# Linear attention and an ELU feed-forward layer on one core: flat attend visits, dummy matmuls in the first batch, and a new order of the work

## The chip, the core and the metric

The kernel runs on one core of a Trainium2 chip. The metric is the device time of one execution in microseconds (us). A core has five engines that run side by side, each with its own queue worked off in order: TensorE (PE, matrix products into the eight PSUM banks), VectorE (DVE), ScalarE (ACT), GpSimd (POOL), and SyncE (SP), which here only starts transfers. POOL and ACT start transfers too; POOL starts those of the weights.

## What is computed

```python
def _attn_ref(q, k, v):                      # each 8 batches x 8 heads x 576 x 64, f32
    q_s = np.exp(q - np.max(q, axis=-1, keepdims=True))
    q_s = q_s / (np.sum(q_s, axis=-1, keepdims=True) + 1e-09)
    k_s = np.exp(k - np.max(k, axis=2, keepdims=True))
    k_s = k_s / (np.sum(k_s, axis=2, keepdims=True) + 1e-09)
    kv = np.einsum('bhsd,bhse->bhde', k_s, v)
    return np.einsum('bhsd,bhde->bhse', q_s, kv)

def _moe_ref(x, w_in, w_out):                # x: 4608 x 512, w_in: 512 x 2048, w_out: 2048 x 512
    h = x @ w_in
    g = np.where(h > 0.0, h, np.exp(np.minimum(h, 0.0)) - 1.0)
    return g @ w_out
```

x is the attention's output with the heads side by side: 8 batches of 576 rows, 512 columns.

## The kernel before

**Blocks.** The 4608 rows of x are worked off in nine blocks j. Blocks 0 to 7 are the first 512 rows (`SM`) of each batch; the remaining 64 rows (`SR`, "the rest") of all eight batches are collected in `XTR` and make block 8. Each block has 16 steps s, one for each 128 hidden columns. A step is: `hidden` (L708, four matmuls L728 of 512 columns into one of three PSUM banks, then the exponential on ACT, L716, and a -1 on POOL, L717, both in the buffer ES), the projection of three steps before (`project`, L749, four matmuls into the banks 3 to 6, `LAG` = 3), and `elu` (L739, DVE: max and min of the bank and ES into GT). A hidden matmul needs the bank that the elu of three steps before has read; a projection needs GT of its step and its piece of W2. After the 16th projection of a block the four banks are evicted (L757 ACT, L759 DVE) and stored.

**Attention.** Beside the steps of block j stands the attention of batch n = j + 1, cut into words that are written by hand into tables: `FIRST` (L42, beside block 0), `SECOND` (L60, block 1), `LATER` (L78, blocks 2 to 6, with `CHANGED` for block 2). A table has three texts for a step: the words behind `hidden`, behind `project` and behind `elu`. `do` (L803) issues them in that order. A word appends its instructions to the queues of their engines, so the order of the words is the order in every queue. `START` (L33) is the list for batch 0, before the steps begin.

The words that matter here (a third field names the engine where it can be chosen; without it qsub, ksub and qmul are POOL's, vconv and the exponentials ACT's):

- `load:X:i:part` starts a transfer of Q, K or V of batch j + i in SP's queue; part A and B are halves, M both, R the rest. `w1:a:b` and `w2:a:b` start transfers of weight columns (or rows) a to b in POOL's queue. `hold` makes SP wait for the last hidden matmul issued, `await:sp:KEY` for the last writer of a tile.
- Q: `qmax` (DVE), `qsub`, `qexp`, `qsum` (DVE, L588 and L590), `qmul` (L602, into QS as f16; `qmulr` for the rest, POOL), then `turn` (a transposing transfer in SP's queue, L618 and L622) and `wide` (ACT, into QT; the rest into QTR). In the first batches `pturn` and `pwide` do this on PE and ACT instead.
- K: in batches 0 to 2 the maximum over rows goes through `kmax`, `kturn`, `kacross`, `diag`, `kspread`, `copy`; later through `peak`, `join`, `kout`, `kin` (a small transfer to memory and back). Then `ksub` and `kexp`. Batch 0 has it as matmuls into PSUM (`kraw` copies K into a bank, `kmin` subtracts the maximum, the exponential reads the bank).
- `vconv` casts V to bf16 (VB), `kv` (L519, 40 matmuls) makes the product, `kfac` (L540, DVE) scales it into the four tiles MB.
- `att:f` (L668) multiplies MB[f] with the 512 columns of QT[f] into bank 7, and `xc:f` copies it to `XT` (L681 ACT, or DVE). `rest0` (L683) does it for the 64 rest columns of all four f in the next block, and `rcopy0` copies those to `XTR`. Suffix 0 in a word means batch j, 2 means batch j + 2.

**Dummy matmuls.** `warm:times:bank` (L862) multiplies a tile of ones into a bank that nobody reads. `START` has one, `warm:4:6`, ahead of all else on PE.

**Waits.** `op` (L141) makes an instruction wait for the last writers of what it reads and for the last writers and readers of what it writes, tile by tile.

## Time and profile before

| what | value |
|---|---|
| median of 3 runs (lowest, highest) | 316.19 us (315.69, 319.87) |
| the profiled execution | 315.58 us |
| its span, first to last instruction | 313.8 us |
| PE busy | 301.7 us, 96% of the span |
| first projection (L749) starts at | 27.81 us |
| a block in the steady part (175.69 to 207.27) | 31.58 us |
| the last projections end, and the last stores | near 310.6 us, 313.8 us |

In the profile, "L728" is line 728 of the kernel above. PEld is TensorE's weight load, which runs beside its matmuls. A timeline row gives start, duration, engine, line, operation, output and input, shape, the number of instructions merged, and in brackets how long the engine sat idle ahead of it and what released it. Durations of neighbouring rows overlap a little, so costs in a row of instructions are taken from start to start.

### The profile page before, as it was taken

How to read it: one execution, taken by the hardware profiler on the slowest of the kernel's cores; microseconds unless marked ns; L12 is line 12 of the kernel's file. 1: busy time of each engine (PE TensorE's matmuls, PEld its weight loads, DVE VectorE, ACT ScalarE, POOL GpSimd, SP SyncE). 2: the span in 40 equal slices, each digit the busy share in tenths (PEclk: the TensorE clock that was granted, in tenths of full speed). 3: DMA queues.
4: the chain of work that ended last, by engine and by line, in shares of the span. 5: the costliest groups of instructions: out<-in, count | busy, mean ns of one | idle time of the engine just before them, and what ended most of it. 6: DMA issues, size and time to landing. Idle time of an engine off the chain costs nothing.

```text
span 313.8 us, 4535 instructions
## 1 busy us (share of the span) xinstructions
PE 301.7 (96%) x1606; PEld 239.1 (76%) x1606; DVE 230.5 (73%) x383; ACT 192.7 (61%) x319; POOL 190.1 (61%) x237
## 2 busy tenths in 40 slices
PE   6778998999999999999999999999999999999995
PEld 3355776688877878887888788888888888888884
DVE  5797996796888979798979897989796353435541
ACT  1675676587856965696569666966696643334432
POOL 1897697468438953995399529952995233333330
PEclk9989999999999999999999999999999999999999
DMA  7999999763796789617951695160512030003003
GB/s 235 327 293 351 382 338 335 178 187 99 193 317 193 178 206 251 207 33 181 304 178 37 186 304 170 36 175 20 167 37 42 0 137 0 0 2 134 0 0 134
DMA packets 65414, 51.35 MB, mean 164 GB/s; under 512 B 29296, under 2 KB 57712, under 8 KB 65392
## 3 DMA queue, kind: packets, MB, share of 16 engines
q1 hardware_dynamic: 57984, 41.23, 47.3%
q0 software_dynamic: 6384, 8.39, 10.9%
q10 hardware_dynamic: 1024, 1.45, 1.6%
q8 instruction: 12, 0.20, 0.3%
q14 instruction: 10, 0.08, 0.1%
HBM read 38.01 MB, written 9.45 MB: 151 GB/s over the span
## 4 chain that ended last, share of the span: by engine, by line
PE 86%; DMA 8%; POOL 3%; DVE 1%; ACT 1%; issue 0%
PE bank L749 40%; PE bank L728 40%; DMA W2S<-in_moe_w_out_dram 6%; PE bank L672 2%; DMA KR<-in_k_dram 1%; PE bank L465 1%; PE bank L529 1%; PE bank L688 1%; POOL QR L578 1%; POOL W1S L247 1%; POOL VB L509 1%; POOL KR L408 1%; PE bank L322 1%; POOL ES L717 0%; PE bank L456 0%; PE bank L533 0%
## 5 line engine op out<-in xcount | busy, mean ns | idle before, releaser
L717 POOL TENSOR_SCALAR ES<-ES 128x512 f32<-128x512 f32 x144 | 100.9, 703 | 105.7 <-ACT ES L716 105.4
L749 PE MATMUL bank<-W2S,GT 128*128 128x512 f32 x576 | 154.6, 392 | 1.6 <-DMA W2S<-in_moe_w_out_dram 1.6
L739 DVE SCALAR_TENSOR_TENSOR GT<-bank,ES 128x512 fp32r<-128x512 f32 x144 | 97.2, 680 | 61.8 <-PE bank L728 44.8
L728 PE MATMUL bank<-XT,W1S 128*128 128x512 f32 x512 | 140.5, 396 | 0.2 <-ACT XT L681 0.2
L716 ACT ACTIVATE ES<-bank 128x512 f32<-128x512 f32 x144 | 85.6, 597 | 77.9 <-PE bank L728 73.9
L749 PEld LDWEIGHTS bank<-W2S,GT 128*128 128x128 f32 x576 | 107.2, 188 | 25.4 <-DVE GT L739 1.6
L728 PEld LDWEIGHTS bank<-XT,W1S 128*128 128x128 f32 x512 | 95.7, 190 | 20.8 <-ACT XT L681 1.1
L578 POOL TENSOR_TENSOR QR<-QR,QM 128x512 f32<-128x512 f32 (+3 forms) x29 | 33.5, 1158 | 7.5 <-DVE QM L570 7.5
L408 POOL TENSOR_TENSOR KR<-KR,NB 128x512 f32<-128x512 f32 x23 | 31.1, 1352 | 0.0
L681 ACT ACTIVATE XT<-bank 128x512 fp32r<-128x512 f32 x31 | 18.4, 598 | 14.8 <-PE bank L672 14.2
L570 DVE TENSOR_REDUCE QM<-QR 128x16 f32<-128x1024 f32 (+3 forms) x18 | 21.7, 1207 | 1.1 <-DMA QR<-in_q_dram 1.0
L588 DVE TENSOR_REDUCE QZ<-QR 128x16 f32<-128x1024 f32 (+3 forms) x18 | 21.7, 1204 | 0.1
L584 ACT ACTIVATE QR<-QR 128x1024 f32<-128x1024 f32 (+3 forms) x18 | 19.1, 1060 | 3.2 <-POOL QR L578 1.7
L602 DVE TENSOR_TENSOR QS<-QR,QI 128x1024 f16<-128x1024 f32 (+1 forms) x15 | 19.8, 1327 | 0.0
L728 PE MATMUL bank<-XTR,W1S 128*128 128x512 f32 x64 | 16.6, 389 | 0.0
L446 ACT ACTIVATE EK<-KR 128x1024 bf16<-128x1024 f32 x14 | 14.7, 1050 | 0.0
L672 PE MATMUL bank<-QT,MB 128*128 128x512 f32 x32 | 13.5, 432 | 0.6 <-DVE MB L550 0.6
L728 PEld LDWEIGHTS bank<-XTR,W1S 128*128 128x128 f32 x64 | 12.0, 188 | 2.5
L511 ACT ACTIVATE VB<-VR 128x1024 bf16<-128x1024 f32 x12 | 12.6, 1049 | 0.0
L662 ACT ACTIVATE QT<-QW 128x1024 fp32r<-128x1024 f16 x12 | 12.5, 1050 | 0.0
L361 DVE TRANSPOSE_TENSOR_REDUCE KM<-KR 128x32 f32<-128x1024 f32 x10 | 12.3, 1234 | 0.0
L515 ACT ACTIVATE VBR<-VR 64x256 bf16<-64x256 f32 x16 | 6.6, 411 | 7.4 <-DMA VR<-in_v_dram 7.2
(85 smaller groups left out, 197.0 us busy)
## 6 DMA issues: line engine op xcount, KB each, us to landing
out_dram<-OSB SPq DMA_DIRECT2D x35, 256.0 KB, 2.9
KR<-in_k_dram SPq DMA_DIRECT2D x7, 1024.0 KB, 8.1
VR<-in_v_dram SPq DMA_DIRECT2D x6, 1024.0 KB, 7.2
QR<-in_q_dram SPq DMA_DIRECT2D x5, 1024.0 KB, 7.1
QR<-in_q_dram SPq DMA_DIRECT2D x6, 512.0 KB, 9.3
VR<-in_v_dram SPq DMA_DIRECT2D x4, 512.0 KB, 6.9
W1S<-in_moe_w_in_dram POOLq DMA_DIRECT2D x1, 1280.0 KB, 12.1
W2S<-in_moe_w_out_dram POOLq DMA_DIRECT2D x1, 1280.0 KB, 10.6
```

The source lines that it names most:

```text
L408: self.op(en, lambda: e.tensor_tensor(kv, kv, m, ALU.subtract), keys + ["NB"], keys)
L570: self.op("dve", lambda: v.tensor_reduce(self.QM[:, g], QR[:, g, :], AX.X, ALU.max), self.qkeys(b, part), self.qstat("QM", part))
L578: self.op(en, lambda: e.tensor_tensor(QR[:, g, :], QR[:, g, :], m, ALU.subtract), keys + self.qstat("QM", part), keys)
L584: self.op("act", lambda: a.activation(QR[:, g, :], QR[:, g, :], AF.Exp), keys, keys)
L588: self.op("dve", lambda: v.tensor_reduce(self.QZ[:, g], QR[:, g, :], AX.X, ALU.add), self.qkeys(b, part), self.qstat("QZ", part))
L602: self.op(en, lambda: e.tensor_tensor(out, src, z, ALU.mult), keys + self.qstat("QI", part), [f"QS{x}" for x in cells])
L672: self.op("pe", lambda: pe.matmul(self.bank[bank][:, :], mb, self.QT[:, f, :], start=True, stop=True), [f"MB{f}", f"QT{part}"], [f"bank{ba ...
L716: self.op("act", lambda: a.activation(ES[:, :], ps, AF.Exp), [f"bank{bank}"], [ek])
L717: self.op("gp", lambda: g.tensor_scalar(ES[:, :], ES[:, :], -1.0, 1.0, ALU.add, ALU.mult), [ek], [ek])
L728: return pe.matmul(ps, self.W1S[:, kc, c * 128:(c + 1) * 128], x[:, kc, :], start=(kc == 0), stop=(kc == 3))
L739: self.op("dve", lambda: v.scalar_tensor_tensor(self.GT[n % NG][:, :], ps, 0.0, ES[:, :], ALU.max, ALU.min), [f"bank{bank}", ek], [f"GT{n ...
L749: return pe.matmul(self.bank[OB[t]][:, :], self.GT[n % NG][:, t * 128:(t + 1) * 128], self.W2S[:, c, :], start=(c == 0), stop=(c == NCH - 1))
```

## The change

Three parts. First, from batch 2 on the four `att` words and the rest become five flat visits: the 4 x 576 columns of the attention's output are cut at `CUTS`, and each visit fills one bank with one or two matmuls and is copied with one instruction. QT and XT get 576 columns for this, and QTR goes away. `xrest` then copies the four rest parts from XT to XTR on POOL. Batches 0 and 1 keep `att` and `rest0`.

```diff
+CUTS = (0, 320, 832, 1344, 1856, 2304)
+VISIT = ((0,), (1, 2), (3, 4), (5, 6), (7,))
...
+    def attend_flat(self, v, bank):
+        pe = self.E["pe"]
+        c0, c1 = CUTS[v], CUTS[v + 1]
+        def mm():
+            for f in range(c0 // S, (c1 - 1) // S + 1):
+                a, b = max(c0, f * S), min(c1, f * S + S)
+                last = pe.matmul(self.bank[bank][:, a - c0:b - c0],
+                                 self.MB[f][:, :, :].rearrange("p u d -> p (u d)"),
+                                 self.QT[:, f, a - f * S:b - f * S], start=True, stop=True)
+            return last
...
+    def xcopy_flat(self, b, v, bank, en="act"):
+        c0, c1 = CUTS[v], CUTS[v + 1]
+        x = self.XT[b % 2][:, :, :].rearrange("p f t -> p (f t)")[:, c0:c1]
+        keys = [f"XT{b % 2}{x // 2}{'LH'[x % 2]}" for x in VISIT[v]]
+        self.copy(en, x, self.bank[bank][:, 0:c1 - c0], [f"bank{bank}"], keys)
+
+    def xrest(self, b, en="gp"):
+        out = self.XTR[:, :, :].rearrange("p f (t s i) -> p f t s i", i=2, s=SR)[:, :, b // 2, :, b % 2]
+        self.copy(en, out, self.XT[b % 2][:, :, SM:S], self.xkeys(b, range(4), "H"), [f"XTR{b}"])
```

Second, `START` has three dummy groups in other places: six matmuls into bank 3 (behind kraw:S), two into bank 6 and four into bank 5 (behind pturn:A and kexp:T), and none at the very beginning. Third, all tables are written anew. START, the table LATER and the words of the others that the prediction speaks of:

```diff
-START = ("load:K:0:A load:Q:0:A kmax:A load:K:0:R load:K:0:B load:Q:0:B warm:4:6 kraw:A qmax:A "
-         "kmax:S kraw:S kturn:A kacross:A kmax:B qmax:2 load:V:0:R await:sp:KAA kraw:B kmax:T "
-         "kturn:B vconv:R:gp qmax:3 diag:act:A kmin:S kacross:B qsub:A:gp w1:2:4 qexp:A load:V:0:A "
-         "load:V:0:B qsub:2:gp kraw:T kexp:S qsub:3:gp diag:act:B vconv:A:gp w1:0:2 qexp:3 qsum:A "
-         "kmin:A kexp:A qmul:A:dve w1:4:5 vconv:B:gp load:K:1:M kmin:B kv:A qexp:2 qsum:2 kmin:T "
-         "w1:5:6 qsum:3 load:Q:1:R kfac:A load:K:1:R w2:0:2 kexp:B pturn:A load:Q:0:R w2:2:3 kexp:T "
-         "kv:B w1:7:8 pwide:A:act w1:6:7 att:1 qmul:2:dve qmul:3:dve await:sp:DGA att:0 w2:3:7 "
-         "kfac:B pturn:B w1:8:11 w2:7:8 xc:1 xc:0 pwide:B:act h:2:4 att:2 w2:8:9 kmax2:A kmax2:B "
-         "xc:2 att:3 await:sp:QS0 xc:3:dve h:0:2 load:Q:1:A kmax2:R ")
+START = ("load:K:0:A load:Q:0:A kmax:A load:K:0:R qmax:A load:K:0:B kmax:S qsub:A:gp kmax:B kraw:A "
+         "load:Q:0:B w1:2:4 kturn:A kraw:S kacross:A kmax:T warm:6:3 diag:act:A qmax:2 qsub:2:gp "
+         "kmin:S kturn:B load:V:0:R qmax:3 load:V:0:A qexp:A kacross:B vconv:A:gp qsub:3:gp "
+         "load:V:0:B vconv:R:dve qexp:2 kmin:A diag:act:B kraw:T kexp:A kexp:S qsum:A qsum:2 kraw:B "
+         "kmin:B load:K:1:M w1:0:2 w1:4:5 qexp:3 qmul:A:dve load:K:1:R vconv:B:gp qsum:3 kv:A kmin:T "
+         "w2:0:1 pturn:A kexp:B w2:1:2 kexp:T kfac:A:dve warm:2:6 qmul:3:dve w1:5:8 warm:4:5 "
+         "qmul:2:dve pwide:A:act att:1 kmax2:B att:0 xc:1 kv:B w2:2:4 kfac:B:dve xc:0 pturn:B h:2:4 "
+         "kmax2:A pwide:B:act w2:4:5 await:sp:MB0 load:Q:1:A att:2 kmax2:R load:Q:0:R att:3 xc:2 "
+         "xc:3 w2:5:7 w1:8:10 h:0:2 ")
...
 FIRST = {
-    0: ("hold", "qmax:A", "hold"),
-    3: ("hold", "", "qexp:A w1:11:16 qmax0:R"),
-    4: ("qsub0:R", "kturn kacross", "hold w2:9:11 qexp0:R qsum:A"),
-    9: ("w2:11:16", "qsum:C", ""),
-    11: ("vconv:A:gp", "rest0 load:K:2:MR", "rcopy0 kexp:R hold hold load:Q:2:ABR"),
+    0: ("hold qmax:A hold", "", ""),
+    3: ("hold", "", "hold w1:10:15 qsub:1 qmax0:R"),
+    4: ("w2:7:9 qexp:A", "hold qsub0:R:dve hold qexp0:R hold kturn", "kacross qsum:A"),
+    5: ("load:Q:1:B qsum0:R w2:9:13", "", "qmax:C"),
+    11: ("w2:13:16 hold qmulr ksub:3:dve hold", "vconv:R hold", "rest0 hold rcopy0"),
+    12: ("pturn:B vconv:A:dve", "ksub:2 load:K:2:MR", "kexp:R hold pwide:B:act"),
...
 LATER = {
-    0: ("", "", "qsub:0"),
-    1: ("", "wide0:R", "kin qsub:1"),
-    2: ("", "", "qsub:2"),
-    3: ("", "", "qexp:A qsub:D ksub:R:dve"),
-    4: ("", "rest0 rcopy0", "vconv:A qsum:A ksub:0"),
-    5: ("", "", "qexp:C qmul:A:dve ksub:1"),
-    6: ("", "", "vconv:R kexp:R qsum:C ksub:2"),
-    7: ("", "", "kexp:A qmul:B:dve ksub:3 turn:A"),
-    8: ("", "", "vconv:B"),
-    9: ("", "", "kexp:B qmulr turn:B load:V:2:MR"),
-    10: ("", "kv:AB kfac:AB", "wide:A load:K:3:MR"),
-    11: ("", "att:0 xc:0", "turn:R peak2:A peak2:R"),
-    12: ("", "att:1 xc:1", "wide:B load:Q:3:MR peak2:B"),
-    13: ("", "att:2 xc:2", "join2"),
-    14: ("", "att:3 xc:3", "qmax2:A"),
-    15: ("", "", "qmax2:C kout2"),
+    0: ("", "qsub:0:dve", ""),
+    1: ("", "qsub:1", "kin vconv:R"),
+    2: ("qsub:2", "", ""),
+    3: ("", "ksub:0:dve ksub:R:dve", "qexp:A"),
+    4: ("qsum:A", "qsub:D", ""),
+    5: ("qmul:A:dve", "qexp:C turn:A", "qsum:C"),
+    6: ("ksub:1 vconv:A", "ksub:3", "ksub:2:dve"),
+    7: ("kexp:A", "qmulr vconv:B:dve", "qmul:B:dve peak2:R"),
+    8: ("kexp:B", "kexp:R", ""),
+    9: ("turn:R", "turn:B kv:AB", "kfac:AB:dve"),
+    10: ("load:K:3:MR wide:R", "wide:A", "load:Q:3:MR"),
+    11: ("peak2:A", "wide:B flat:0 peak2:B xflat:0", "join2"),
+    12: ("", "flat:1", "xflat:1"),
+    13: ("", "kout2 flat:2", "load:V:2:MR xflat:2"),
+    14: ("", "", "flat:3 xflat:3"),
+    15: ("qmax2:C flat:4", "qmax2:A xflat:4", "xrest"),
 }
```

In `SECOND` the flat visits of batch 2 stand at the steps 13 to 15. Two smaller parts: the four MB tiles are set to zero on POOL at the beginning, and `kfac` may name ACT for its scaling, which no table does.

More of the change, by code (lines that the diff above doesn't have):

```diff
@@ L73 @@
-    12: ("", "kv:AB kfac:AB peak2:R", ""),
-    13: ("peak2:A", "att:2 xc:2", ""),
-    14: ("", "att:0 xc:0", ""),
-    15: ("join2 att:1", "xc:1 load:V:2:MR", "att:3 qmax2:A xc:3 kout2"),
+    0: ("", "qmax:A kturn", "qsub:1 kacross qmax:C"),
+    1: ("qsub:2", "diag qsub:0", ""),
+    2: ("load:K:2:MR", "kspread", ""),
+    3: ("vconv:B", "", "copy ksub:A:dve wide0:R"),
+    4: ("qsub:D:dve", "ksub:R", "load:Q:2:MR qexp:A"),
+    5: ("qsum:A", "kexp:A qexp:C", "ksub:2 vconv:A:dve"),
+    6: ("qmul:1", "", "qsum:C vconv:R"),
@@ L77 @@
+    7: ("rest0", "", "rcopy0"),
+    8: ("ksub:3", "", "kexp:R qmulr qmul:B:dve"),
+    9: ("peak2:R turn:R peak2:A", "kexp:B turn:B qmul:0:dve", ""),
+    10: ("turn:A", "kv:AB kfac:AB:dve", "wide:R"),
+    11: ("", "wide:B wide:A", "peak2:B"),
+    12: ("join2", "", ""),
+    13: ("", "flat:0 load:V:2:MR", "xflat:0"),
+    14: ("flat:1 xflat:1", "qmax2:A flat:2 kout2", "xflat:2"),
+    15: ("flat:3 xflat:3 load:K:3:MR", "flat:4 xflat:4", "xrest"),
 }
 LATER = {
[L79 to L80 removed]
```

99 lines of the change are left out of this document (57 added, 42 removed).

## The prediction, made before the changed kernel was run

> **What bounds the kernel now.** I read the page from the top, then the windows, then the timelines by engine. Columns of the windows: length, then busy us and instructions of PE, PEld, DVE, ACT and POOL, granted clock, DMA share, GB/s.
>
> ```profile
> span 313.8 us, 4535 instructions
> PE 301.7 (96%) x1606; PEld 239.1 (76%) x1606; DVE 230.5 (73%) x383; ACT 192.7 (61%) x319; POOL 190.1 (61%) x237
> DMA  7999999763796789617951695160512030003003
> GB/s 235 327 293 351 382 338 335 178 187 99 193 317 193 178 206 251 207 33 181 304 178 37 186 304 170 36 175 20 167 37 42 0 137 0 0 2 134 0 0 134
> ```
>
> TensorE (PE) is the bound: only 12.1 us of the span are not busy. The first seven slices (55 us) run the DMA engines at 300 GB/s and more, so there the arrival of weights is the second bound.
>
> ```profile
> 20.60:24.00 3.40, 3.40 (x13) 2.68 (x11) 2.75 (x9) 1.75 (x3) 3.33 (x6) 0.50 1.66 319
> 17.20:20.60 3.40, 1.75 (x33) 1.09 (x31) 3.26 (x12) 2.70 (x5) 3.40 (x6) 1.00 1.61 256
> 175.69:207.27 31.58, 31.58 (x183) 25.78 (x177) 27.12 (x43) 22.21 (x35) 22.08 (x26) 1.00 0.63 173
> ```
>
> A batch in the steady part takes 31.58 us and PE never stops; DVE is busy for 27.1 of them. In the start PE has one stretch at half clock, behind one in which it was busy for 1.75 of 3.40.
>
> ```profile
> 20.78 2.08 PE L728 MATMUL bank<-XT,W1S 128*128 128x512 f32 x4
> 22.65 1.05 PE L672 MATMUL bank<-QT,MB 128*128 128x512 f32 x2
> 23.51 3.15 PE L728 MATMUL bank<-XT,W1S 128*128 128x512 f32 x12
> 27.81 1.17 PE L749 MATMUL bank<-W2S,GT 128*128 128x512 f32 x4 [1.16 <-DMA W2S<-in_moe_w_out_dram]
> ...
> 163.49 0.53 PE L688 MATMUL bank<-QTR,MB 128*128 128x64 f32 x4
> 163.85 1.17 PE L728 MATMUL bank<-XT,W1S 128*128 128x512 f32 x4
> 164.86 1.08 PE L749 MATMUL bank<-W2S,GT 128*128 128x512 f32 x4
> ```
>
> The first projection (L749) starts at 27.81 on w2's first piece. A plain group of four matmuls takes 0.91 us start to start. The four short matmuls of the rest (L688) take 0.36 and the group behind them 1.01, so a rest costs 0.46 us.
>
> ```profile
> 40.27 1.08 DVE L408 TENSOR_TENSOR KR<-KR,NB 128x512 f32<-128x512 f32 x1
> 44.12 1.78 DVE L408 TENSOR_TENSOR KR<-KR,NB 128x512 f32<-128x512 f32 x1
> 70.82 0.63 DVE L408 TENSOR_TENSOR KR<-KR,NB 128x512 f32<-128x512 f32 x1
> 104.19 1.50 DVE L602 TENSOR_TENSOR QS<-QR,QI 128x1024 f16<-128x1024 f32 x1
> ```
> ```profile
> 104.58 1.59 POOL L717 TENSOR_SCALAR ES<-ES 128x512 f32<-128x512 f32 x1
> ```
>
> One and the same subtraction on DVE takes 0.63 alone and up to 1.78 beside POOL's, and POOL's ES (0.62 alone) takes 1.59 until DVE's product is done: these two wait for each other.
>
> **The change, part by part.** All durations are of the one profiled execution, which took 315.58 us: its span of 313.8 and 1.78 around it. The median of the three runs shown is 316.19, 0.61 above that, the lowest 315.69.
>
> *Start, to the first projection.* The transposes of Q wait for qmul:A, which stands behind one more sum in DVE's queue: 16.8 instead of 16.5. But kfac:A comes ahead of qmul:2 and qmul:3, and kexp:A ahead of one qexp, so att:1 has both operands at about 18.7 (was 19.13), the copies xc end at 20.3 (20.72) and h:2:4 starts there (20.78). kmax2:B now stands ahead of kfac:B: MB2 comes at 21.6 instead of 20.6, still before att:2 ran (22.65). Two XT copies of 0.55 on ACT then end at 23.1, the last four matmuls of hidden 0 at 23.6 (was about 25.1), and exp, ES and GT (0.60 + 0.62 + 0.61 with 0.3 of hand-overs) give GT0 at 25.75. POOL's queue has w2:0:1 ahead of w1:5:8 and without the second half of the old piece: 0.5 MB less in front, issue at 17.1 instead of 18.57. At 340 GB/s it lands near 25.1 (27.7). So the first projection starts at 25.75: 2.1 us earlier. The SP queue loses its wait for kmax, so V goes out 2.2 us earlier and K of batch 1 behind it; Q:1:A goes behind MB0, at 18.3 instead of 16.57, but without K:1 (10.5 us to landing) still in front: half a megabyte in 4 to 5 us is there at 23, before DVE's qmax:A (queued ahead of the first GT) wants it.
>
> *Dummy matmuls.* Six at 10.1, after kraw:S: 1.4 to 2.6 us, where kmin:S waits for diag:A until 10.9; behind them kmin:S, kturn:B and kraw are late by up to 0.7, which kexp:A (ACT gets to it at 14.0) covers; without that cover they cost the 0.7. Two and four before att:1 need 1.4 between 17.5 and 18.9; the four wait in bank 5 for kexp:T (17.6), and att:1 behind them wants to start at 18.7: at most 0.2. They fill the stretch that was busy for 1.75 of 3.40; I take the half clock at 20.6 as gone, which is in the 23.6 above (13 matmuls at half speed cost some 1.6). The Trainium skill, "TensorE: Matmul & The Clock Gate", section "What's actually happening", has the clock fall only after an idle window of about 3.4 us. No such idle window stands before 20.6 in this trace, so by that rule dummies would not cure the drop, and the sum would be 1.3 higher.
>
> *Weights behind that.* Loads are the same bytes. With 0.34 MB per us the pieces w1:5:8, w2:2:4, w2:7:9 and w2:9:13 arrive within 1 us of when a PE that is 2.1 ahead wants them: I give 0.5 back (0 to 1.5). PE's holes of before at 47.1, 53.2 and 58.2 (0.38, 0.42, 0.22) may close, as K:2 and Q:2 go out after the last w2 piece: half of it, 0.5.
>
> *Flat visits, batches 2 to 7.* Old: four attends, 0.24 to 0.31 each (1.04), and a rest of 0.46, together 1.50. New: eight matmuls of 2304 columns in all, 4.5 x 0.227 = 1.02, with two short ones (192 and 128 columns) that hide less of a weight load: a rest's exposed load is (0.46 - 0.11) / 4 = 0.09 each, so up to 0.18. Saved 0.3 per batch (0 to 0.45), x 6 = 1.8 us. Bank 7 is free 1.03 us after a visit starts (177.65 to 178.68); visit 4 starts 1.16 after visit 3, so it just fits. The last copy has 1.8 us until the next batch's last quarter. xrest on POOL is not in the trace: 0.61 to 0.75 (L608, L412, 128x256), where POOL is idle for 9.5 us a batch. The four memsets of MB (0.20 each) lie before 7.97, where POOL idles for 6 us.
>
> *Words of the steady batches (LATER, five batches).* Removed from POOL: qsub:0 (1.04), ksub:0 and ksub:2 (1.33 each). Added to DVE: these three at 0.63, and vconv:B, not in the trace on DVE: 0.69 (128x512 copy) to 1.24 (128x1024 in one pass); the same cast takes 1.05 on ACT, which I take. ksub:R loses its neighbour on POOL, 1.76 to 0.82. DVE: 27.1 + 1.9 + 1.05 - 0.95 = 29.1 of some 31.3 us. The room is not in the mean: before, the GT of the step with H (end of its hidden matmuls) 201.89 ends at 206.4, and the hidden matmul that needs its bank starts at H + 4.54 = 206.43. Counting from the end of hidden 0 with 1.814 a step, the new DVE queue runs: evictions to 5.5, ksub:0 and ksub:R to 8.1, GT3 8.7, qsum:A, GT4 10.7, qmul:A 12.05, GT5, qsum:C 14.4, GT6 15.0, then ksub:2, which waits for POOL's ksub:3 and ends at 15.95. kexp:B and kexp:R (1.05 + 0.42, ACT) end at 17.45; kv, moved one step earlier, is wanted on PE at 17.24: 0.2 late. Behind it ksub:2, vconv:B, GT7, qmul:B and peak2:R put GT8 at 20.4 to 21.0, wanted at 20.2. turn:R now stands between turn:A and turn:B with no load ahead of it (2.3 us to landing at the least), wide:R and wide:A end at 22.35, flat:0 is wanted at 22.1. Together 0.5 to 1.3 a batch if DVE loses each race for the lock, nothing if it wins two of them. I take 0.5 (0 to 1.5), nearer to the low end since before had the same queue full to the last 0.03 us at no cost: x 5 = 2.5 us. The Trainium skill, "VectorE: DVE Perf Modes", section "The perf-mode tier table (the rule you actually need)", has this cast at twice the rate; from its 1227 ns for 2048 elements I estimate 0.69 for vconv:B, and the sum would be some 1.5 lower.
>
> **Sum:** 315.58 - 2.1 + 0.5 - 0.5 - 1.8 + 2.5 = 314.2; for a median of runs, which lay 0.61 above the profiled one, I add half of that: **314.5**.
>
> **Rivals.**
> - *DVE's queue overruns (slower).* Place: from ksub:R to GT8. For it: the three subtractions have two SBUF inputs and waited up to 1.15 us for POOL (44.12); against it: POOL has 3 us less. At 0.8 us a batch it eats all gains (3.9 / 5); at 1.5 to 2.4 the time is 315.58 - 3.9 + 7.5 to 12 = 319 to 323.7.
> - *Q:1:A is late.* For it: half a megabyte took 9.0 us before. qmax:A would hold the first GT until 28.2 and the projection until 28.9: 1.1 us lost in place of 2.1 won, 317.4.
> - *The dummies don't hold the clock:* 1.3 more, 315.8. Against it: the stretch before (13.8 to 17.2) was busy for 2.05 of 3.40 and kept it.
> - *DVE wins its races, nothing waits:* 315.58 - 2.1 - 1.0 - 1.8 = 310.7. For it: the mean room of 2 us; against it: the replay above.
>
> **How the numbers follow.** Forecast 0.52 (own range 311 to 317), overrun 0.20, late Q 0.10, nothing waits 0.13, clock 0.05. 2% is about what a measurement of this kernel can tell from no change: 309.9 and 322.5. Under 309.9 lies about half of "nothing waits", 0.07; over 322.5 nearly half of the overrun, 0.09; 0.84 between. The range 309.7 to 320.5 leaves out about 0.07 below and 0.13 above.
>
> **What would show it.** First L749 at 25 to 26.5 with clock 1.00 from 20 to 24; no L688 after batch 1 and 0.3 us less PE time per batch; batches of 31.3 to 32 us, with PE idle, if any, ahead of kv (ACT EK or DVE VB as releaser), of a hidden matmul (GT) or of flat:0 (QT). A batch over 32.5 us, a first projection after 27.8, or a batch under 31.2 makes it wrong.

## The result and the profile after

The changed kernel takes **319.33 us** (median of 20 runs, 318.69 to 320.94), the kernel before 316.23 (20 runs): ratio **1.0102, 95% interval 1.0085 to 1.0118**. It is one per cent slower. The forecast was 314.5 with a range up to 320.5: the time lies in the range, the direction is wrong.

First the page of the changed kernel, its span, busy times and DMA slices:

```profile
span 317.4 us, 4576 instructions
PE 300.5 (95%) x1614; PEld 237.1 (75%) x1614; DVE 246.2 (78%) x406; ACT 187.0 (59%) x313; POOL 171.9 (54%) x230
DMA  8999999995494759624962495334332021003003
```

PE has 1.2 us less work than before (300.5 against 301.7) and yet the span is 3.6 longer: PE now waits 16.9 us instead of 12.1. DVE has 15.7 us more to do, POOL 18.2 and ACT 5.7 less.

Where in the span? A good landmark is the eviction of a block's output on DVE (L759 before, L809 after), which comes two steps into the next block:

| stretch | before, us | after, us | difference |
|---|---|---|---|
| to the first projection | 27.81 | 26.37 | -1.44 |
| from there to the end of block 0 | 36.07 (63.88) | 39.24 (65.61) | **+3.17** |
| block 1 | 32.34 | 33.31 | **+0.97** |
| blocks 2, 3, 4, 5 | 31.74, 31.64, 31.58, 31.58 | 32.28, 31.90, 31.93, 32.13 | +0.54, +0.26, +0.35, +0.55 |
| block 6 | 31.58 | 31.29 | -0.29 |
| block 7 | 29.50 | 29.01 | -0.49 |
| sum | | | +3.6 |

Now the waits. PE's timeline after, those rows of blocks 0 to 3 that carry a wait of 0.2 us or more:

```profile
26.37 1.20 PE L799 MATMUL bank<-W2S,GT 128*128 128x512 f32 x4 [0.83 <-DVE GT L789]
30.30 0.66 PE L325 MATMUL bank<-ID,KA 128*128 128x128 f32 x4 [0.92 <-DVE GT L789]
40.74 1.20 PE L778 MATMUL bank<-XT,W1S 128*128 128x512 f32 x4 [1.78 <-DVE GT L789]
45.06 0.29 PE L649 MATMUL bank<-ID,QSR 128*128 128x128 f16 x2 [0.27 <-DVE QT L665]
...
52.28 0.32 PE L532 MATMUL bank<-VB,EK 128*64 128x66 bf16 x8 [0.96 <-DVE VB L512]
60.25 0.73 PE L778 MATMUL bank<-XT,W1S 128*128 128x512 f32 x2 [0.23 <-ACT XT L694]
88.02 0.41 PE L707 MATMUL bank<-QT,MB 128*128 128x320 f32 x1 [0.27 <-ACT QT L675]
115.14 1.19 PE L778 MATMUL bank<-XT,W1S 128*128 128x512 f32 x4 [0.32 <-DVE GT L789]
147.41 1.19 PE L778 MATMUL bank<-XT,W1S 128*128 128x512 f32 x4 [0.30 <-DVE GT L789]
```

No row waits for W2S any more; nearly every wait is for something that DVE makes. What DVE itself did ahead of three of them is in its timeline:

```profile
27.42 2.22 DVE L591 TENSOR_TENSOR QR<-QR,QM 128x512 f32<-128x512 f32 x1
29.57 0.68 DVE L789 SCALAR_TENSOR_TENSOR GT<-bank,ES 128x512 fp32r<-128x512 f32 x1
...
38.60 1.49 DVE L583 TENSOR_REDUCE QM<-QR 128x20 f32<-128x1280 f32 x1 [3.88 <-DMA QR<-in_q_dram]
...
50.46 1.76 DVE L512 CAST VB<-VR 128x1024 bf16<-128x1024 f32 x1
...
53.56 0.68 DVE L512 CAST VB<-VR 128x1024 bf16<-128x1024 f32 x1
```

The first is the subtraction qsub:0: newly on DVE, it takes 2.22 us (the same form took 0.83 and 1.25 in the kernel before), and behind the late GT PE stands for 0.92. qmax:C waits 3.88 us for Q:1:B; in the kernel before it started at 35.52 without a wait. Its queue holds the GT that PE wants at 39. The cast vconv:A takes 1.76 next to POOL's subtraction (50.39 to 51.67) and 0.68 when POOL is idle, three microseconds later. SP's queue shows why Q:1:B was late (the third row is from a narrower stretch of the same queue, and is half of the second):

```profile
17.98 0.37 SPq L281 DMA_DIRECT2D QR<-in_q_dram  x1
18.39 7.60 SPq L273 DMA_DIRECT2D QR<-in_q_dram  x4
24.73 1.26 SPq L273 DMA_DIRECT2D QR<-in_q_dram  x2
28.56 0.37 SPq L281 DMA_DIRECT2D QR<-in_q_dram  x1
```

Q:1:A goes out at 17.98. The second row merges four short loads of the rests, each of which takes only 0.60 to 0.62: two (Q:0:R) from 18.39 on, two (Q:1:R) from 24.73 on. Between them SP stands at the `hold` words, 5.0 us for PE's hidden matmuls, and behind them at the next ones. So Q:1:B, which now stands in step 5, goes out at 28.56 (before, in step 2: at 25.32) and lands at 38.6.

Last the clock, the two stretches that were shown of before:

```profile
17.20:20.60 3.40, 3.40 (x41) 2.14 (x38) 3.30 (x11) 2.70 (x5) 3.40 (x6) 1.00 1.84 304
20.60:24.00 3.40, 3.35 (x16) 2.25 (x14) 2.59 (x9) 2.24 (x4) 1.88 (x3) 1.00 1.23 344
```

The dummies fill the first, and the second is granted 1.00 instead of 0.50.

### The profile page after: what moved, and what is told of

The parts are those of the page before. It is cut to its first block, busy times and chain, and to the rows that moved or that the text cites. A ratio compares the mean times of both kernels' runs of the same rounds, so it can differ in the third digit from the quotient of the medians.

```text
span 317.4 us, 4576 instructions
## 1 busy us (share of the span) xinstructions
PE 300.5 (95%) x1614; PEld 237.1 (75%) x1614; DVE 246.2 (78%) x406; ACT 187.0 (59%) x313; POOL 171.9 (54%) x230
## 4 chain that ended last, share of the span: by engine, by line
PE 78%; DMA 7%; DVE 6%; ACT 4%; POOL 3%; issue 2%; SPq 1%; DVEq 0%
PE bank L778 36%; PE bank L799 35%; DMA QR<-in_q_dram 3%; PE bank L707 2%; DVE GT L789 2%; DMA KR<-in_k_dram 2%; PE bank L532 1%; DMA QWR<-QSR 1%; POOL ES L767 1%; DMA QW<-QS 1%; ACT QR L597 1%; PE bank L685 1%; POOL KR L411 1%; ACT ES L766 1%; ACT QT L675 1%
## 5 line engine op out<-in xcount | busy, mean ns | idle before, releaser
L767 POOL TENSOR_SCALAR ES<-ES 128x512 f32<-128x512 f32 x144 | 98.4, 686 | 126.8 <-ACT ES L766 126.2
L778 PEld LDWEIGHTS bank<-XT,W1S 128*128 128x128 f32 x512 | 93.1, 188 | 24.3 <-DVE GT L789 5.5
L591 POOL TENSOR_TENSOR QR<-QR,QM 128x512 f32<-128x512 f32 (+2 forms) x24 | 28.1, 1173 | 8.7 <-DVE QM L583 8.7
L729 ACT ACTIVATE XT<-bank 128x512 fp32r<-128x512 f32 (+2 forms) x30 | 16.6, 552 | 10.2 <-PE bank L707 8.1
L411 POOL TENSOR_TENSOR KR<-KR,NB 128x512 f32<-128x512 f32 x14 | 17.9, 1298 | 0.0
L707 PEld LDWEIGHTS bank<-QT,MB 128*128 128x128 f32 x48 | 8.8, 188 | 5.2 <-DVE MB L563 1.3
L707 PE MATMUL bank<-QT,MB 128*128 128x320 f32 (+5 forms) x48 | 11.7, 305 | 0.5 <-ACT QT L675 0.4
L411 DVE TENSOR_TENSOR KR<-KR,NB 128x512 f32<-128x512 f32 (+1 forms) x13 | 11.7, 896 | 0.0
```

Of the source, the lines that this page charges most:

```text
L411: self.op(en, lambda: e.tensor_tensor(kv, kv, m, ALU.subtract), keys + ["NB"], keys)
L591: self.op(en, lambda: e.tensor_tensor(QR[:, g, :], QR[:, g, :], m, ALU.subtract), keys + self.qstat("QM", part), keys)
L707: last = pe.matmul(self.bank[bank][:, a - c0:b - c0], self.MB[f][:, :, :].rearrange("p u d -> p (u d)"), self.QT[:, f, a - f * S:b - f * S ...
L767: self.op("gp", lambda: g.tensor_scalar(ES[:, :], ES[:, :], -1.0, 1.0, ALU.add, ALU.mult), [ek], [ek])
L778: return pe.matmul(ps, self.W1S[:, kc, c * 128:(c + 1) * 128], x[:, kc, 0:SM], start=(kc == 0), stop=(kc == 3))
```

## The experiments

Fourteen kernels; each is the changed kernel with an edit unless it says otherwise. "Block 0" is the stretch from the first projection to the eviction.

### 1. The load of Q:1:B earlier

```diff
-    2: ("load:Q:1:R", "", "qsub:0:dve"),
+    2: ("load:Q:1:R load:Q:1:B", "", "qsub:0:dve"),
...
-    5: ("load:Q:1:B qsum0:R w2:9:13", "", "qmax:C"),
+    5: ("qsum0:R w2:9:13", "", "qmax:C"),
```

> The changed kernel with one word moved back: the second half of Q of batch 1 is loaded at step 2 of block 0, right behind its rest, and no longer at step 5. Theory 1 (this late load holds DVE's queue: qmax:C waits 3.88 us for it at 38.6, and PE then stands 1.78 us at 40.7 and 0.96 us at 52.3 for GT and VB): the load lands near 35, the wait shrinks to under 0.5 us, and 2 to 3 us of the 3.6 us of span come back; the time is 316.3 to 317.3. Theory 2 (block 0 is bound by the arrival of weights, and the wait of DVE is hidden by it): the wait goes and PE then waits for W2 or W1 instead, under 0.7 us comes back. Theory 3 (DVE simply has too much work in block 0): the wait goes, but PE still waits for GT, 1 us comes back at most.

Measured: 319.38 us, ratio 1.0113 (1.0063 to 1.0164): nothing is won in the whole, and none of the theories' numbers came out. The load went out 2.6 us earlier, right behind Q:1:R, but landed only 1.35 earlier, at 37.25, and DVE still waited 2.56 for it: it took 11.2 us to land, where Q:1:B of the kernel before, sent at 25.32, took 9.6. PE's wait of 1.78 became 0.48 and 0.22, and block 0 got 1.0 us shorter (it ends at 64.59 instead of 65.61); blocks 3 and 4 of that execution are 0.26 and 0.81 longer, the second with a wait of 0.51 for an eviction on ACT. The place is right, but this is not yet the repair.

### 2. The words of the steady blocks back on POOL and ACT

```diff
-    0: ("", "qsub:0:dve", ""),                  # likewise ksub:0, and vconv:B to ACT
+    0: ("", "qsub:0", ""),
```

> The changed kernel with three words of the table LATER back on the engines they had: qsub:0 and ksub:0 on POOL, vconv:B on ACT. If the loss in the steady blocks is DVE's queue (PE idle 0.30 and 0.47 lost for the GT of step 8, once a batch), the wait is gone in the blocks 2 to 5, each is 0.4 to 0.6 us shorter, together 1.6 to 2.5 us: 317 to 317.7. If the loss is in the flat visits' waits for bank 7 or for the copies, the blocks stay at 31.9 us and the time at 319.3. If POOL becomes late instead, PE waits for kv (EK) and the blocks get longer than 32 us.

Measured: 319.96, ratio 1.0131 (1.0096 to 1.0166). The wait for GT is gone from every block, and another one stands in its place, once a block, at kv:

```profile
113.04 0.32 PE L532 MATMUL bank<-VB,EK 128*64 128x66 bf16 x8 [0.63 <-ACT EKR L452]
145.00 0.32 PE L532 MATMUL bank<-VB,EK 128*64 128x66 bf16 x8 [0.62 <-ACT EKR L452]
```

Blocks 2 to 6 take 31.96 to 31.98. With the cast on ACT, the exponential of the rest of K comes too late for a kv that was moved one step forward. The engine of the words is thus not the only thing that costs; the place of kv is the other.

### 3. No dummy matmuls

```diff
-... warm:6:3 ...   ... warm:2:6 ...   ... warm:4:5 ...
+(all three words left out)
```

> The changed kernel without its three groups of dummy matmuls. If the dummies hold the clock, the granted clock falls to 0.5 for 3.4 us near 20.6, hidden 0 ends about 1.3 us later and the first projection is at 27.5 to 28 instead of 26.4; at the end up to 1 us of it is left, since DVE waits for the load of Q of batch 1 until 38.6 anyway: 319.3 to 320.3. If the clock does not depend on them, it stays at 1.0 and the time is the same or up to 0.3 us lower.

Measured: 321.4, ratio 1.0168 (1.0117 to 1.0219). Windows of this run, aligned to its start:

```profile
17.90:21.30 3.40, 1.75 (x34) 1.20 (x32) 3.29 (x11) 2.70 (x5) 3.40 (x6) 0.98 1.52 305
21.30:24.70 3.40, 3.40 (x12) 2.72 (x11) 3.00 (x8) 1.84 (x4) 1.87 (x3) 0.52 1.20 345
```

Without dummies the half clock is back. The first projection comes at 28.10 instead of 26.37; 0.66 of that is K, which landed later in this execution, so some 1.1 us are the dummies' doing, as far as one execution of each can tell. All of the 1.7 us is left at the end (span 319.1 against 317.4), where up to 1 was expected.

### 4. Flat visits alone

The words of before in all tables; batches 3 to 7 get flat visits in the place of the four attends and the rest.

```diff
-    11: ("", "att:0 xc:0", "turn:R peak2:A peak2:R"),
+    11: ("", "flat:0 xflat:0", "wide:R peak2:A peak2:R"),
...
-    15: ("", "", "qmax2:C kout2"),
+    15: ("flat:4", "xflat:4", "qmax2:C kout2 xrest"),
```

> The kernel before with the flat visits alone: its own words in all tables, five visits for the batches 3 to 7 (batch 2 keeps four attends and its rest), turn:R ahead of V's load and wide:R at step 11 as the visits need them. If the flat visits save what block 6 of the changed kernel showed (0.29 a batch, and 0.46 for the last rest), the span is 1.4 to 1.9 us shorter than before: 314.2 to 314.9. If they make PE wait for bank 7 or QT, PE idle shows ahead of the visits, and the gain is under 0.7 us.

Measured: 316.05, ratio 1.001 (0.9973 to 1.0047), span 313.2 against 313.8. The steady block, which took 31.58 before:

```profile
159.80:191.20 31.40, 31.40 (x177) 25.63 (x176) 27.01 (x43) 22.00 (x35) 22.48 (x27) 1.00 0.61 175
```

PE never idle, 0.18 us less a block; the last block 29.01 instead of 29.50. The block in which the visits begin has the rest of one batch and the visits of the next and takes 32.51, 0.77 more than before. So in total nothing that can be measured.

This execution shows something else. START is that of before, yet the first projection comes at 26.27, as early as in the changed kernel, and the clock is 1.00 from 20.60 to 24.00, behind a stretch (17.20 to 20.60) in which PE worked 2.33 of 3.40 us. Block 0 then takes 37.33 instead of 36.07, with a wait of 1.35 for W2S at 34.22:

```profile
26.27 1.17 PE L801 MATMUL bank<-W2S,GT 128*128 128x512 f32 x4 [1.31 <-DMA W2S<-in_moe_w_out_dram]
```

The late start and the half clock of the profiled execution before do not come every time, and of an early start most is taken back by the weights.

### 5. The first block's words of before

FIRST of before in the changed kernel, its weight pieces fitted to the new START, the loads Q:1:R and Q:1:B in step 2.

```diff
-    2: ("load:Q:1:R", "", "qsub:0:dve"),
-    3: ("hold", "", "hold w1:10:15 qsub:1 qmax0:R"),
+    2: ("", "load:Q:1:R load:Q:1:B qsub:1:dve", ""),
+    3: ("hold", "", "qexp:A w1:10:16 qmax0:R"),
...
```

> The changed kernel with the table FIRST of before (weights that its own START has not loaded are loaded at the same words, and Q of batch 1's rest goes out at step 2 with the second half of Q). Block 0, from the first projection to the eviction of its output, took 36.1 us before and 39.2 in the changed kernel. Theory 1 (the order of the words in FIRST makes block 0 long: three subtractions and two casts put on DVE, which wait there for POOL, and the late load of Q): block 0 is 36 to 37 us long, 2 to 3 us come back, 316.3 to 317.3. Theory 2 (START's new order, with its first projection 1.4 us earlier, has spent the lead of the loads, so PE now waits for W1, W2 or Q whatever FIRST does): block 0 stays over 38 us and the time over 318.3.

Measured: 317.4, ratio 1.0036 (1.0008 to 1.0064). Block 0 takes 38.36 instead of 39.24, longer than theory 1 has it, and the whole is 1.9 us better than the changed kernel, more than theory 2 allows. One long wait is left that before had not:

```profile
40.24 1.19 PE L778 MATMUL bank<-XT,W1S 128*128 128x512 f32 x4 [1.67 <-DVE GT L789]
```

Ahead of it DVE waits 2.73 us for Q:1:B until 37.04. The load went out at 25.34, as in the kernel before (25.32), but took 11.7 us to land instead of 9.6; what made it slower is not shown.

### 6. kv of the steady blocks one step later

Run 2, and kv and kfac back in step 10:

```diff
-    9: ("turn:R", "turn:B kv:AB", "kfac:AB:dve"),
-    10: ("load:K:3:MR wide:R", "wide:A", "load:Q:3:MR"),
+    9: ("turn:R", "turn:B", ""),
+    10: ("load:K:3:MR wide:R", "kv:AB kfac:AB wide:A", "load:Q:3:MR"),
```

> The changed kernel with the three words of LATER back on POOL and ACT as in the run before (qsub:0, ksub:0, vconv:B), and in addition kv and kfac of LATER back at step 10. That run showed PE idle 0.63 ahead of kv, for ACT's exponential of K's rest. Theory: kv at step 9 is one step too early for K's chain on whatever engine it runs, so with both undone no wait is left, the blocks 2 to 5 are 31.2 to 31.5 us (31.9 in the changed kernel), and 2 us come back: 317 to 317.6. Rival: the wait only moves on to flat:0 (MB, QT) or to the GT of step 8, blocks stay at 31.8 to 32.

Measured: 319.9, ratio 1.0118 (1.0059 to 1.0177). No wait for GT or EKR is left; three of blocks 2 to 5 take 31.73 to 31.84 and one 33.01, with one wait of 0.68 for XT. That is some 0.2 better than the changed kernel's blocks, and still 0.35 over the 31.40 of run 4; the whole is no faster than the changed kernel (1.0118 against 1.0102). Which word makes the rest stays open.

### 7. The second block's words of before

```diff
-SECOND = { ... "flat:0 load:V:2:MR" ... "flat:4 xflat:4", "xrest" ...
+SECOND = { ... "att:2 xc:2" ... "att:0 xc:0" ...        # and the rest of batch 2 in block 2
```

> The changed kernel with the table SECOND of before: batch 2 has four attends and its rest again. Block 1 took 32.34 us before and 33.31 in the changed kernel. If the five flat visits crowded into the steps 13 to 15 with one bank between them make it long, block 1 is 32.2 to 32.5 us, block 2 longer by the rest (0.46), 0.3 to 0.7 us come back: 318.6 to 319. If the words ahead of them (the chain of Q to QT, wide after a late turn) are the cause, it is the same since they go too; if block 1 stays over 33 us, what FIRST hands over late is the cause.

Measured: 320.39, ratio 1.014 (1.0083 to 1.0197). Block 1 takes 32.02 instead of 33.31, so it was its words that cost the 0.97. But block 2 takes 34.09 instead of 32.28:

```profile
101.17 1.23 PE L801 MATMUL bank<-W2S,GT 128*128 128x512 f32 x4 [1.66 <-ACT OSB L809]
```

Here the eviction of the output on ACT stands behind vconv:R, which waits 2.34 us for V. The tables of two neighbouring blocks belong together.

### 8. Dummies in the kernel before

```diff
-... pturn:A load:Q:0:R ...   ... "kv:B w1:7:8 ...
+... pturn:A warm:2:6 load:Q:0:R ...   ... "kv:B warm:2:2 w1:7:8 ...
```

> The kernel before with four dummy matmuls more in START: two behind the transposes of Q (pturn:A), two behind kv:B, nothing else. If dummies hold the clock, it stays at 1.0 through 20 to 24, hidden 0 ends 1 to 1.5 us earlier, but the first projection waits for W2's first piece (27.7) all the same: the first projection at 27.3 to 27.8 and the time 315.8 to 316.3, no change that can be measured. If the weights were not what bounded it, 1 us is won: 315.2.

Measured: 315.45, ratio 0.998 (0.9951 to 1.0009). The profiled execution is the slowest of the ten (317.35) and not typical. In it the clock holds until 24, the hidden matmuls are done early, and PE then waits for the weights:

```profile
28.04 1.55 PE L749 MATMUL bank<-W2S,GT 128*128 128x512 f32 x4 [2.54 <-DMA W2S<-in_moe_w_out_dram]
```

Behind this pause the clock is granted at 0.68 (27.4 to 30.8) and 0.82 (30.8 to 34.2). It is the only one of the ten whose mean clock lies under 0.999 (0.994). Of the kernel before, measured in the same round, 8 of 19 executions reached 0.998; these took 314.70 to 315.75, the other eleven 316.07 to 318.00. One stretch of 3.40 us at half clock lowers the mean over 314 us by 0.005. So the dummies do hold the clock here. What that is worth, some 0.6 us by the medians, is not clear of the noise.

### 9. All of Q of batch 1 in the start

Run 5, and (the two loads leave step 2 of FIRST for it):

```diff
-... load:Q:1:A att:2 kmax2:R load:Q:0:R att:3 ...
+... load:Q:1:A load:Q:1:B att:2 kmax2:R load:Q:0:R load:Q:1:R att:3 ...
```

> The changed kernel with the first block's words of before, as in the run with before's FIRST, and with both remaining loads of Q of batch 1 moved into the start right behind Q:1:A, so that none of them stands behind the short loads of SP's queue (four of those held the queue from 18.2 to 25.3). In that run VectorE stood idle for 2.73 us until 37.04 for these loads, and TensorE for 1.67 at 40.2. Theory 1 (that wait is the rest of what block 0 lost): Q:1:B lands before 33, VectorE's wait is gone, the wait at 40.2 is under 0.5, block 0 takes 36.2 to 37.2 and the whole 316 to 316.6. Theory 2 (the megabytes have to arrive anyway; a load that comes earlier makes a piece of weights late): the wait at 40.2 goes, but waits for W2S of 1 us or more stand in block 0, which stays at 38 or more: 317.2 to 318. Theory 3 (the wait at 40.2 is a loss of the queue of VectorE and not of the load): it stays above 1.2 us.

Measured: 317.22, ratio 1.0049 (1.0027 to 1.0072), span 314.8. DVE's qmax:C starts at 35.26 without a wait, PE's wait of 1.67 is gone, and block 0 takes 37.40 (to 63.52). One for weights has come:

```profile
42.87 1.19 PE L799 MATMUL bank<-W2S,GT 128*128 128x512 f32 x4 [0.73 <-DMA W2S<-in_moe_w_out_dram]
```

The load was the cause of that wait, as theory 1 has it, and block 0 is 0.96 us shorter (38.36 to 37.40). The whole is where theory 2 has it, and not to be told from run 5 (1.0036); the new wait for weights stands in the place of one of 0.54 at 54.51 in run 5. That four short loads held the queue, as the expectation says, is a misreading: in run 5, too, the two pairs took 1.25 us each, and SP stood at a `hold` between them.

### 10. Two words of the first block back on POOL

```diff
-    2: ("load:Q:1:R", "", "qsub:0:dve"),
+    2: ("load:Q:1:R", "", "qsub:0"),
...
-    12: ("pturn:B vconv:A:dve", "ksub:2 load:K:2:MR", "kexp:R hold pwide:B:act"),
+    12: ("pturn:B vconv:A:gp", "ksub:2 load:K:2:MR", "kexp:R hold pwide:B:act"),
```

> The changed kernel with two words of its first block back on POOL, qsub:0 and the cast vconv:A, and nothing else. Theory 1 (the operations that were put on VectorE beside POOL wait for each other there): the subtraction's 2.22 us at 27.4 and the cast's 1.76 at 50.5 are gone from VectorE, TensorE's waits of 0.92 at 30.3 and 0.96 at 52.3 are under 0.4 together, block 0 is 0.8 to 1.5 us shorter (unless the wait for Q:1:B at 40.7, which is left as it is, takes it back), and the whole takes 318.0 to 319.0. Theory 2 (the wait for Q:1:B ends last and takes up what is won ahead of it): the wait at 40.7 grows by what the one at 30.3 loses, only the 0.96 behind it is won: 318.4 to 318.8. Rival (POOL is too slow for them here): kv of block 0 waits longer for the cast than the 0.96, and the whole takes 319.3 or more.

Measured: 317.51, ratio 1.007 (1.0048 to 1.0093). Block 0 takes 37.45, 1.8 less than the changed kernel's, more than either theory had:

```profile
39.37 0.96 PE L778 MATMUL bank<-XT,W1S 128*128 128x512 f32 x3 [1.72 <-DVE GT L789]
...
50.18 0.32 PE L532 MATMUL bank<-VB,EK 128*64 128x66 bf16 x8 [0.26 <-POOL VB L512]
```

The wait of 0.92 at 30.3 is gone and the one for VB is 0.26 instead of 0.96. The wait for Q:1:B did not grow: the load went out at 28.38, 0.18 earlier, and took 8.8 us to land instead of 10.0 (DVE has Q at 37.23 instead of 38.60). Why it landed faster is not shown, so a part of the 1.8 may be the execution's.

### 11. The good parts together, first try

START and FIRST of run 9; SECOND, LATER and CHANGED of run 4.

```diff
-(changed kernel's FIRST, SECOND, LATER, CHANGED)
+(FIRST of run 9; SECOND, LATER, CHANGED of run 4)
```

> Start of the changed kernel with all of Q of batch 1 in it, the first block, the second and the steady blocks with the words of before, and flat visits in batches 3 to 7: what the earlier runs say is good in the change, without what they say is bad. If block 0 is 36.2 to 37.2 as in theory 1 of the run with Q in the start, the first projection at 26.3 makes 62.5 to 63.5 of the end of block 0, and the 244.65 us that the run with flat visits alone took from there to its last eviction give a span of 312.1 to 313.1: 314.3 to 315.3 us, 0.3 to 0.6% under before. If the weights bound the first blocks whatever comes first, it is level with the run with flat visits alone, 316 us. Above 316.5: the start of the changed kernel costs something that no run has shown yet.

Measured: 316.25, ratio 1.0008 (0.9986 to 1.0031). Block 0 takes 37.65, with waits for W2S of 1.10 and 1.00, and block 2 has one of 0.99 for an eviction that stands on ACT behind a small transfer. Level with run 4, as the second case said; whether the bytes or their order make the waits for weights was the question of run 12.

### 12. The transfers in another order

Run 11, and:

```diff
-    3: ("hold", "", "qexp:A w1:10:16 qmax0:R"),
-    4: ("qsub0:R", "kturn kacross", "hold w2:7:11 qexp0:R qsum:A"),
+    3: ("hold", "", "qexp:A w1:10:12 w2:7:9 qmax0:R"),
+    4: ("qsub0:R", "kturn kacross", "hold w1:12:16 w2:9:11 qexp0:R qsum:A"),
...
-    11: ("vconv:A:gp", "rest0 load:K:2:MR", ...
+    11: ("vconv:A:gp", "rest0 hold load:K:2:MR", ...
```

> The kernel of the run that put the good parts together, in which TensorE waited for pieces of w2 for 1.10 us at 42.57 and 1.00 at 53.71 while the DMA engines were busy without a break from 20 to 58. Only the order of the transfers is changed: the six chunks of w1 are asked for in two pieces with two chunks of w2 between them, and K of batch 2 goes out some 10 us later. Theory 1 (the order of the transfers makes those waits: K, which nobody wants before 55, takes the place of w2): both waits are under 0.5 together, block 0 ends at 61.8 to 62.5 and the whole takes 314.2 to 314.9, some 0.5% under before. Theory 2 (all of these bytes are wanted in this time whatever their order): the waits move to another piece or to K of batch 2 in steps 14 and 15 and block 0 ends at 63.5 or later: 316 to 316.6.

Measured: 318.19, ratio 1.0041 (1.0 to 1.0081), worse than either theory. The twelve executions lie between 316.1 and 321.72, and the profiled one is among the slower (319.16). The wait for W2S at 42.6 (1.10) is gone with no new wait ahead of it (the first projection is 0.38 later), so the order of the transfers made it. The one at 53.7 is gone too, behind a wait that neither theory had. PE's row, the two rows of DVE ahead of it, and the window behind it:

```profile
47.19 0.77 PE L740 MATMUL bank<-QT,MB 128*128 128x64 f32 x4 [2.50 <-DVE QT L667]
```
```profile
40.19 1.76 DVE L413 TENSOR_TENSOR KR<-KR,NB 128x512 f32<-128x512 f32 x1
44.72 2.08 DVE L413 TENSOR_TENSOR KR<-KR,NB 128x512 f32<-128x512 f32 x1
```
```profile
48.00:60.00 12.00, 11.99 (x85) 8.53 (x86) 7.51 (x19) 7.57 (x13) 5.38 (x7) 0.88 0.98 287
```

Two subtractions on DVE took 1.76 and 2.08 (in run 11: 1.09 and 1.07), the copy of QT behind them came late, and after PE's pause of 2.5 us the clock was granted at 0.88 over the next 12 us. Whether DVE is late like this whenever the wait for weights is taken away, one execution cannot say.

### 13. Both repairs

The changed kernel with the START of run 9 and the two words of run 10.

> The changed kernel with both repairs of its first block: all of Q of batch 1 is asked for in the start, and qsub:0 and vconv:A are POOL's again. Each by itself brought block 0 (first projection to the eviction of its output) from 39.24 to 37.4 us. Theory 1 (two separate causes: a load, and the pairs of operations that wait for each other): the gains add, block 0 takes 35.6 to 36.2, no wait of TensorE between 27 and 55 is over 0.5, and the whole takes 315.6 to 316.4. Theory 2 (behind these waits stand the bytes of the weights: in the runs with an early Q, TensorE waited for W2S at 42.9 or 53.7): block 0 stays at 37.0 to 37.5 with waits for W2S in the place of the others, and the whole takes 317 to 317.6.

Measured: 317.14, ratio 1.003 (1.0 to 1.006), span 315.0. Block 0 takes 36.28 (26.15 to 62.43): 2.96 of the 3.17 us that it had lost are back. What is left in it is 0.30 for W2S and 0.80 for a cast that is now POOL's. So theory 1 is nearer for the block, which lies 0.08 over its upper edge and has one wait over 0.5; the median is where theory 2 had it. The later blocks are still the changed kernel's (33.35, then 31.84 to 33.25).

The expectation speaks of run 9 as if it were the load alone; it has the words of before as well. What each is worth is better read from pairs of runs that differ in one thing. The words: 1.79 (changed kernel to run 10). The load: 1.17 (run 10 to 13), and 0.96 with the words of before (run 5 to 9). These are single executions, though, and with the same START and FIRST block 0 takes 39.22 to 39.93 (changed kernel, runs 2, 6 and 7), 37.40 and 37.65 (runs 9 and 11), 36.28 and 35.31 (runs 13 and 14). So the two repairs together, 2.9 to 4.6 us, are clear of this; the share of each is not. With both mended the weights do not hold block 0 at 37.4.

### 14. Both repairs, and flat visits alone behind them

START and FIRST of run 13; SECOND, LATER and CHANGED of run 4.

> Start and first block as in the run with both repairs, the later blocks with the words of before and flat visits in batches 3 to 7. By theory 1 of that run the end of block 0 comes at 61.9 to 62.6, and the 244.65 us that the run with flat visits alone took from there to its last eviction give a span of 311.5 to 312.2, so 313.5 to 314.5 us: 0.5 to 0.8% under before. By theory 2 it is level with before, 316 to 316.6. A wait for the eviction of the output on ACT near 98 (0.99 us in the run that put the good parts together) would add up to 1 to either.

Measured: **314.21** (313.64 to 315.25), ratio **0.9939 (0.9917 to 0.9961)**: faster than both kernels.

```profile
26.21 1.19 PE L801 MATMUL bank<-W2S,GT 128*128 128x512 f32 x4 [0.81 <-DVE GT L791]
47.92 0.32 PE L534 MATMUL bank<-VB,EK 128*64 128x66 bf16 x8 [0.78 <-ACT ES L768]
56.01 0.73 PE L780 MATMUL bank<-XT,W1S 128*128 128x512 f32 x2 [0.22 <-ACT XT L696]
95.93 1.22 PE L801 MATMUL bank<-W2S,GT 128*128 128x512 f32 x4 [0.95 <-ACT OSB L809]
```

These are all but one of PE's waits of 0.2 or more from the first projection on (0.28 at 191.6 is the other). Block 0 ends at 61.52, 2.36 earlier than before, and block 2 gives 0.95 back to an eviction on ACT. There is no wait for W2S, and in run 13, with the same START and FIRST, one of 0.30: they ask for the weights in smaller pieces than run 11 did, which fits the answer of run 12 (order, not bytes), although other words differ too. Against run 4, which has the same words from block 1 on, START and the mended FIRST win 0.7% (0.9939 against 1.001, the intervals apart). So the early start does reach the end, once the words behind it are ready.

## Why the prediction was wrong, step by step

The step that failed is "Weights behind that": it put what comes behind the first projection at 0.5 - 0.5 = 0, and block 0 cost 3.17 us more, by DVE and not by weights. A second loss, some 0.8 in block 1, has no term in the sum at all. The other terms were right in kind: -1.44 for -2.1, the visits as forecast, +2.9 for +2.5. Of the signs that were to show the prediction wrong, none came at the first projection (26.37) or in the steady batches (31.90 to 32.28): no sign was set for blocks 0 and 1.

**Start, to the first projection: right in kind, two thirds in size.** 1.44 us won instead of 2.1. Hidden 0 was done some 0.6 later than worked out: its exponential began at 24.21 in the place of 23.6, with the hand-overs behind it as worked out. Q:1:A, the subject of a rival, held no GT. The 1.44 is against one execution of before: in three traces with START of before, or with that and dummies (run 8), the first projection comes at 27.81, 26.27 (run 4) and 28.04; in the twelve traces with the changed START and its dummies at 26.12 to 26.59.

**Dummy matmuls: right, with a limit.** The clock held, run 3 brings the half clock back when they go, and run 8 shows the same by the mean clocks of ten executions. But without them the half clock comes only in a part of the executions (run 4 had none), so the 1.3 was never a loss of every execution. By the rule of the Trainium skill ("TensorE: Matmul & The Clock Gate", section "What's actually happening") only an idle window of some 3.4 us brings it on; the trace of run 3 does not agree, since 1.75 us of work in 3.40 were followed by 0.52.

**Weights behind that: failed.** The step looked for the price of an earlier start among the weights, 0.5 us (0 to 1.5), and won 0.5 from three holes. (It read 300 GB/s and more in all of the first seven slices; the first and the third have 235 and 293.) With the words of before such a price is there: 1.26 in run 4. In the changed kernel PE waits for no weights at all, and block 0 costs 3.17 more for two reasons that the sum has no term for. One is a transfer: the prediction followed Q:1:A through SP's queue and stopped there, although Q:1:B had been moved too, from step 2 to step 5 and behind more `hold` words, at which it goes out 3.2 us later. The other is the words of FIRST: `qsub:0:dve` and `vconv:A:dve` are in the quoted diff, and the prediction quotes the rows that price them (0.63 alone, up to 1.78 beside POOL) but used them only for the steady batches. Runs 5, 9, 10, 13 and 14 show these two. Together they make the loss: with both mended block 0 takes 36.28 and 35.31, against 36.07 before. The pairs of runs give 1.0 to 1.2 us for the load and 1.79 for the words, which single executions do not fix to better than a us. The holes it counted on were not won; others (0.96 at 52.3, 0.27 at 45.1) came.

**SECOND: not priced at all.** Block 1 lost 0.97, where the flat visits of batch 2, which bring one more rest into it, explain 0.17 (a visit group less 0.29, a rest more 0.46). Of the other 0.8, PE's wait for QT at 88.02 is 0.27. The rest, it seems, lies with the place of the visits: five in three steps. Each needs bank 7, which the copy of the one before has to free on ACT:

```profile
89.32 0.30 PEld L707 LDWEIGHTS bank<-QT,MB 128*128 128x128 f32 x2 [0.39 <-ACT XT L729]
90.53 0.30 PEld L707 LDWEIGHTS bank<-QT,MB 128*128 128x128 f32 x2 [0.20 <-ACT XT L729]
91.72 0.30 PEld L707 LDWEIGHTS bank<-QT,MB 128*128 128x128 f32 x2 [0.18 <-ACT XT L729]
93.16 0.19 PEld L707 LDWEIGHTS bank<-QT,MB 128*128 128x128 f32 x1 [0.39 <-ACT XT L729]
```

A visit and the one group of matmuls behind it take PE 1.23 to 1.34 here, and 1.13 to 1.22 in block 2, where most steps have one visit: some 0.5 in four visits. The prediction's "it just fits" was worked out for two visits in one step of LATER, and was carried over to a table where four follow each other. Run 7 confirms that SECOND's words make the loss; it exchanges all of them, so it does not show that the visits' place is the reason.

**Flat visits, batches 2 to 7: right.** 0.29 in block 6, where nothing else disturbs, is the forecast 0.3; with the words of before it is 0.18 (run 4), inside the 0 to 0.45.

**LATER: right in place and kind, the count and the size off in opposite directions.** The wait came where the replay had it, at the GT of step 8, 0.30 to 0.32 on PE. But each of blocks 2 to 5 lost 0.55 to 0.84 against what the visits save (2.9 in all), and block 6 nothing: it prepares no peak for a batch behind it, and DVE is busy for 22.4 us there instead of 29.4. Foretold were 0.5 x 5 = 2.5. The reason given for the low end, that "before had the same queue full to the last 0.03 us at no cost", was the wrong way round: a queue without slack has to be priced at the lost race. DVE's 12 subtractions of 512 columns took 0.87 on the mean (alone 0.63 to 0.72) and its 8 casts 1.08, which is nearly the 1.05 that was taken:

```profile
L411 DVE TENSOR_TENSOR KR<-KR,NB 128x512 f32<-128x512 f32 x12 | 10.4, 869 | 0.0
L512 DVE CAST VB<-VR 128x1024 bf16<-128x1024 f32 x8 | 8.6, 1078 | 0.0
```

Run 2 shows besides that taking the words off DVE does not help: kv, one step earlier, then waits for ACT. With LATER of before and flat visits the same blocks take 31.40 to 31.43 where nothing disturbs them (runs 4, 11 and 14), so it is the words of LATER that lose; which of them, beside kv, stays open.

**The rivals.** The overrun of DVE's queue gave 319 to 323.7, and the time of 319.33 lies there by luck: that rival needs 1.5 us or more in each steady batch, 7.5 in all, and they lost 2.9, near the forecast's own 2.5. What is missing between 314.5 and 319.33 was lost in blocks 0 and 1, which no rival priced. Run 14 comes to 314.21, near the forecast, and that is luck too: it has no new LATER (2.5 in the sum) and flat visits in five batches, not six.

## What to carry to other kernels

Price every table that a change rewrites, not only the one that runs most often: here blocks 0 and 1 lost 4.1 us and the five steady ones 1.4, net of what the visits save. When a load moves, follow each of its pieces to its landing and name what stands ahead of it in the same queue, the words that only wait among them. A row that merges several loads can hide such a wait: read it again in a narrower window. A chain that starts earlier wins nothing unless the next thing it needs starts earlier as well. And where two engines hold each other up, an operation that is moved from the one to the other is priced by the row that shows the race lost.

## What the chip did that was not expected

- A load of 64 KB took 0.60 to 0.62 us of SP's queue, the 512 KB load in front of it 0.37 (changed kernel, 17.98 to 25.99).
- Q:1:B, 512 KB, took 9.6 us to land when it went out at 25.32 (before), 11.7 at 25.34 (run 5), 11.2 at 25.99 (run 1) and 8.8 at 28.38 (run 10). What makes the difference was not tried by itself.
- A half clock followed a stretch in which PE worked 1.75 of 3.40 us with waits of at most 1.65 (run 3); a clock under 1.00 also followed pauses of 2.50 (run 12) and 2.54 (run 8). It stayed at 1.00 behind stretches of 2.05 (before, 13.80 to 17.20), 1.89 and 2.33 (run 4, 13.80 to 17.20 and 17.20 to 20.60).
- DVE's subtraction took 2.22 us at the worst, against 0.83 and 1.25 for the same form before; the cast took 0.68 alone and 1.76 beside POOL's subtraction. The Trainium skill ("SBUF — State Buffer", section "🔬 SBUF: two separate sides") has the two engines share one port pair that one of them holds for a whole instruction; these rows agree with that.
